# A decode kernel's row change: layer 1 one V tile earlier, and longer FFN steps

## The chip, the cores and the metric

The kernel runs on one core of one Trainium2 chip. The metric is the device time of one execution in microseconds (us). Each kernel was timed beside the kernel before on the same chip, in alternating rounds.

Words used below. PE is the engine of the matrix products, DVE and ACT are the vector and the scalar engine, SP issues the loads; PSUM is the buffer that products are written to. A *tile* is the keys (K) or values (V) of two heads of one batch row, 2 MB. A *unit* is a quarter of a tile, 512 KB, 4 KB in each of 128 partitions. The *arena* is the SBUF buffer of 26 units into which all cache data is loaded. A *visit* is the work on two heads of one row in one layer. A *turn* is the stretch in which layer 0 of a row ends, its feed-forward network (FFN) runs, and layer 1 of that row starts; there are eight. A *gap* is the place in PE's instruction order between the products of two units, where the planner puts small work.

## The reference, cut to what matters

```python
# B=8 rows, one token each, D=640, 32 heads of 128, 4096 cached keys, Dff=1728, bf16
x = A_x
x = x + attention(layernorm(x), k_cache, v_cache, wq, wo)     # layer 0
x = x + relu(layernorm(x) @ w1) @ w2
x = x + attention(layernorm(x), k_cache, v_cache, wq, wo)     # layer 1: same cache, same weights
x = x + relu(layernorm(x) @ w1) @ w2
```

Both layers read the same cache of 537 MB. Layer 1 of a row needs the whole of layer 0 and the FFN of that row first. Rows do not depend on each other, so while row b is between its layers, the kernel works on the first heads of row b+1.

## The kernel before

A planner in Python writes one list of operations for all engines ahead of time. The parts that matter are cut out here ("# ..." marks cuts).

```python
UNIT = 4; G = 26; SPARE = 5; STASH = 3; AHEAD = 2; CAP = 20

def plan(B, NP, n_up, n_down):
    # visits: 16 visits of layer 0 of row b+1, of which the first AHEAD=2 come before layer 1 of row b
    # ...
    keep = set(first[: G - SPARE])               # 21 units stay in the arena from layer 0 for layer 1
    stash = first[G - SPARE : G - SPARE + STASH] # 3 more are copied aside
    slots = []
    for i in range(NV + 1):
        pair = [("K", i)] * (i < NV) + [("V", i - 1)] * (i >= 1)
        ends = i and visits[i - 1][0] == 0 and last_of[visits[i - 1][:2]] == i - 1
        turns = 0 < i < NV and visits[i][0] == 1 and visits[i - 1][0] == 0
        slots += pair[::-1] if ends or turns else pair
    # ...
    def release(which, i, g):      # PE is done with a unit: its place is free, and feed() issues loads
        # ... kept units of layer 0 are not freed
        owner[u], freed[u] = False, at[1]
        # ...
        feed()

    def step():                    # one gap: the next piece of every open chain, up to CAP products
        n, now = 0, []
        for c in sorted(chains, key=lambda c: c[0][0]):
            if not n or n + c[0][0] <= CAP:
                n += c[0][0]; now.append(c)
        # ...

    def finish(layer, b):          # the FFN of a row as a chain of steps (number of products, name)
        # ...
        for k in range(n_up):      # 5 steps of 15 products
            c += [own(15, "up", k)]
            # ...
        c += [own(0, "relu")] + [own(14, "down", k) for k in range(n_down)] + [own(0, "add")]
        c += [own(2, "mean"), own(0, "center")] + query(b, 0)   # next query of the row
        c += [own(1, "var2"), own(0, "root2")] + query(b, 1)
        return c

# the loads and the products of a K unit near a turn
def do_load(b, p, n, u):
    nc.sync.dma_start(out=arena[:, u * GW : (u + n) * GW], in_=A_kv[b, :, p * GW : (p + n) * GW])
# ... keys as weights: 16 products of 128x128 by 128x1 a unit
for n in range(4 * c, 4 * c + 4):
    nc.tensor.matmul(s_tiles[i][:, j : j + 1], lhsT=arena[:, at + n * P : at + (n + 1) * P],
                     rhs=qo[:, b, h : h + 1], start=True, stop=True)
```

What this makes of a turn: 21 units of the row that is ending stay in the arena for layer 1, which saves loading them again. Only 5 places are left for the stream. From the first tile ahead until layer 1 starts to free kept units, each load waits for PE to finish the unit five places back. I call this the *ring*. I call *lead* the time from the issue of a load (the end of the instruction that issues it) to the landing of the load ahead of it: it says how much work the DMA engines still have queued when the new load arrives. In the plan a middle turn (row 1) runs: K tiles of two visits ahead (8 gaps), V tile of the first, V tile of the second, then layer 1's first K tile, which is kept.

Of the kernel before, what the change touches and what calls it, by code (L numbers as in the profile page):

```python
# [22 lines left out]
SOON = 4  # L23
PACE, LATE = 0.6, 2
PAD = 2048
AHEAD = 2
BANK = 512
CAP = 20


def tile_at(NP, which, hp):

    return max(0, 2 * hp - 1) if which == "K" else min(2 * hp + 2, 2 * NP - 1)


def plan(B, NP, n_up, n_down):



# [5 lines left out]
    visits = [(0, 0, hp) for hp in order0]  # L45
    for b in range(B - 1):
        nxt = [(0, b + 1, hp) for hp in order0]
        cur = [(1, b, hp) for hp in order1]
        if b + 1 < B - 1:
            visits += nxt[:AHEAD] + cur + nxt[AHEAD:]  # L50
        else:
            visits += nxt[:AHEAD] + cur[: NP - AHEAD] + nxt[AHEAD:] + cur[NP - AHEAD :]
    visits += [(1, B - 1, hp) for hp in order1]
    NV = len(visits)
    assert NV == 2 * B * NP and NP % GP == 0
    turns = [visits.index((1, b, order1[0])) for b in range(B)]
    moving = [not any(t - AHEAD - 1 <= i < t + 5 for t in turns) and i < NV - 2 for i in range(NV)]
    last_of = {(layer, b): v for v, (layer, b, hp) in enumerate(visits)}
    direct = [i == NV - 1 or visits[i][0] == 0 and last_of[visits[i][:2]] == i for i in range(NV)]
    ahead = [next((t - i for t in turns if 0 < t - i <= AHEAD), 0) for i in range(NV)]  # L60

# [7 lines left out]
    slots = []  # L69
    for i in range(NV + 1):  # L70
        pair = [("K", i)] * (i < NV) + [("V", i - 1)] * (i >= 1)
        ends = i and visits[i - 1][0] == 0 and last_of[visits[i - 1][:2]] == i - 1
        turns = 0 < i < NV and visits[i][0] == 1 and visits[i - 1][0] == 0
        slots += pair[::-1] if ends or turns else pair
    stream, uses = [], []
    for which, i in slots:
        layer, b, hp = visits[i]
# [17 lines left out]
    ops, chains, done = [], [], set()  # L95
# [81 lines left out]
    def step():  # L177
# [3 lines left out]
        for c in sorted(chains, key=lambda c: c[0][0]):  # L181
            if not n or n + c[0][0] <= CAP:
                n += c[0][0]
# [11 lines left out]
    def query(b, n):  # L195

        return [(10, ("Q", b, order1[n])), (0, ("QC", b, order1[n]))]
# [9 lines left out]
    def finish(layer, b):  # L207

        def own(n, *op):
            return n, ("C", layer, b, *op)  # L210

        c = []
        for k in range(n_up):
            c += [own(15, "up", k)]
            if layer:
                c += [own(0, "relu", k)]
            elif k == min(1, n_up - 1):
                c += [own(0, "var"), own(0, "root")]
        if layer:
            for k in range(n_up):  # L220
                c += [own(15, "down", k)] + [own(0, "var"), own(0, "root")] * (k == n_up // 2)
            return c + [own(0, "add")]
        c += [own(0, "relu")] + [own(14, "down", k) for k in range(n_down)] + [own(0, "add")]
        c += [own(2, "mean"), own(0, "center")] + query(b, 0)
        c += [own(1, "var2"), own(0, "root2")] + query(b, 1)
        return c

    feed()
    for which, i in slots:
        layer, b, hp = visits[i]  # L230
# [66 lines left out]
def kernel(  # L297
# [15 lines left out]
    B, Sq, D = A_x.shape  # L313
    H = A_wo.shape[1] // D
    NP = H // 2
    Dh = A_kv.shape[1]
    W = (A_kv.shape[2] - PAD) // (2 * NP)
    Sk = W // 2
    Dff = B_w1.shape[1] // (D // P)
    assert Sq == 1 and Dh == P and D % P == 0 and W % (UNIT * P) == 0  # L320
    DC = D // P
# [6 lines left out]
    FC = (Dff + P - 1) // P  # L328
# [73 lines left out]
    ends = consts.tile([P, 2, B, DC], BF16, name="ends")  # L402
# [18 lines left out]
    assert len(stash) > DC  # L421
    nc.vector.memset(o_ps, 0.0)

    up_parts = [range(f, min(f + 3, FC)) for f in range(0, FC, 3)]
    visits, moving, direct, ahead, ops = plan(B, NP, len(up_parts), DC)
    s_tiles, P_rows, P_tiles, m_tiles, o_tiles, oy, invL, oT, nmax, st = ({} for _ in range(10))

    def first_norm(xln):
# [61 lines left out]
    def over_partitions(out, t):  # L490
        for k in range(2):
            nc.tensor.matmul(out, lhsT=ones_p, rhs=t[:, :, k], start=(k == 0), stop=(k == 1))
# [38 lines left out]
    def finish_steps(layer, b):  # L531




        b0, nb = (b, 1) if layer == 0 else (0, B)
        x = xT[:, b0 : b0 + nb, :]
        if layer:
            h = [(ffn_ps if k % 2 else s_ps)[:, : FC * nb].rearrange("p (f b) -> p f b", b=nb) for k in range(len(up_parts))]
            y = stash_ps.bitcast(FP32).rearrange("p (c n) -> p c n", n=BANK)[:, :DC, :nb]  # L540
        else:
            h = [ffn_ps[:, :FC].rearrange("p (f b) -> p f b", b=1)] * len(up_parts)
            y = ffn_ps[:, FC * B : FC * B + DC].rearrange("p (c b) -> p c b", b=1)

        def up(k):
            for f in up_parts[k]:
                fs = f_sizes[f]
                for c in range(DC):
                    nc.tensor.matmul(
                        h[k][:fs, f, :], lhsT=w1_sb[:, c, f * P : f * P + fs], rhs=st["xf"][:, :, c],  # L550
                        start=(c == 0), stop=(c == DC - 1),
                    )

        def var():
            over_partitions(var_ps[:, :nb], st.pop("s2"))

        def var2():
            over_partitions(var2_ps, st.pop("s2"))

        def root():  # L560
            if layer:
                st["rstd"] = root_of_all(var_ps[:, :nb])
            else:
                st["rstd"] = sm.tile([P, 1], FP32, name="rstd", bufs=1)
                inverse_root(st["rstd"], var_ps[:, :1], 1.0)

        def relu(k=None):
            if not k:
                st["hT"] = temp([P, nb, FC], BF16, "hT").rearrange("p b f -> p f b")
            part = range(FC) if k is None else up_parts[k]  # L570
            for rows, lo, hi in ((P, part[0], min(part[-1] + 1, n_full)), (Dff % P, n_full, part[-1] + 1)):
                if rows and lo < hi:
                    nc.vector.tensor_scalar(
                        out=st["hT"][:rows, lo:hi], in0=h[k or 0][:rows, lo:hi], scalar1=0.0, scalar2=None, op0=ALU.max
                    )

        def down(k):
            for c, f in [(k, f) for f in range(FC)] if layer == 0 else [(c, f) for f in up_parts[k] for c in range(DC)]:
                fs = f_sizes[f]
                nc.tensor.matmul(  # L580
                    y[:, c, :], lhsT=w2_sb[:fs, f, c * P : (c + 1) * P], rhs=st["hT"][:fs, f, :],
                    start=(f == 0), stop=(f == FC - 1),
                )

        def add():
            yT = y.rearrange("p c b -> p b c")
            if layer == 0:
                nc.vector.scalar_tensor_tensor(out=x, in0=yT, scalar=st["rstd"], in1=x, op0=ALU.mult, op1=ALU.add)
                s1 = sm.tile([P, 1], FP32, name="s1", bufs=1)
                nc.vector.tensor_reduce(out=s1, in_=x, axis=AX.X, op=ALU.add)  # L590
                st["s1"] = halves(s1, "s1h")
                return
            t = temp([P, nb, DC], FP32, "ffn")
            nc.vector.tensor_tensor(out=t, in0=yT, in1=_free(st["rstd"], [(1, nb), (0, DC)]), op=ALU.mult)
            nc.vector.tensor_tensor(out=outT, in0=x, in1=t, op=ALU.add)

        def mean():
            over_partitions(mean2_ps, st.pop("s1"))

        def center():  # L600
            xc = sm.tile([P, 1, DC], FP32, name="xc", bufs=1)
            nc.vector.scalar_tensor_tensor(
                out=xc, in0=_free(mean2_ps, [(1, 1), (0, DC)]), scalar=-1.0 / D, in1=x, op0=ALU.mult, op1=ALU.add
            )
            xlns[b] = sm.tile([P, 1, DC], BF16, name="xq", bufs=2)
            nc.vector.tensor_copy(out=xlns[b], in_=xc)
            st["s2"] = halves(squares(xc), "s2h")

        def root2():
            r = q_scale[b] = sm.tile([P, 2], FP32, name="q_scale", bufs=2)  # L610
            inverse_root(r[:, 0:1], var2_ps, float(Dh))
            nc.gpsimd.tensor_scalar(out=r[:, 1:2], in0=r[:, 0:1], scalar1=-1.0, scalar2=None, op0=ALU.mult)

        return dict(up=up, var=var, root=root, relu=relu, down=down, add=add, mean=mean, center=center, var2=var2, root2=root2)
# [58 lines left out]
    def do_mm(which, i, g, u):  # L673
# [19 lines left out]
        for c in range(4):  # L693
            if moving[i]:
# [5 lines left out]
                continue  # L700
            s_tiles[i] = o_ps[:, 2 * NJ : 4 * NJ] if ahead[i] == AHEAD else s_ps[:, i % 2 * 2 * NJ : (i % 2 + 1) * 2 * NJ]
            h = 2 * hp + c // 2
# [164 lines left out]
def _laid_out(A_x, A_k_cache, A_v_cache, A_wq, A_wo, B_w1, B_w2):  # L867
# [12 lines left out]
    for hp in range(NP):  # L880
        kv[:, :, tile_at(NP, "K", hp)] = k[:, hp]
        kv[:, :, tile_at(NP, "V", hp)] = v[:, hp]
    kv = np.pad(kv.reshape(B, p, -1), ((0, 0), (0, 0), (0, PAD)))
    return {
# [32 lines left out]
```

## Time and profile before

Before: 2340.57 us median of 3 runs (2338.99 to 2340.59). Lines of the page of the kernel before (the head and parts 2, 3, 4 and 6; part 2 has 40 slices of some 59 us; the last line tells loads of one unit, their number and the median time from issue to landing):

```profile
span 2343.0 us, 43024 instructions
...
GB/s 411 430 433 401 433 432 432 431 396 432 432 432 430 404 434 431 430 427 403 433 432 431 426 412 434 430 432 420 427 431 427 432 416 430 431 431 431 396 433 329
DMA packets 76753, 990.87 MB, mean 423 GB/s; under 512 B 8596, under 2 KB 8596, under 8 KB 36500
...
q8 instruction: 146, 2.39, 0.4%
...
DMA 71%; PE 17%; ACT 6%; DVE 3%; issue 2%; SPq 0%; POOL 0%; ACTq 0%; DVEq 0%; POOLq 0%
...
arena<-in_A_kv_dram SPq DMA_DIRECT2D x218, 512.0 KB, 6.5
```

DMA bounds the kernel: the chain of waits is 71% arrival of data, and the rate is 426 to 434 GB/s in the slices without a turn, the first and the last slice aside. The Trainium skill, "DMA: Bandwidth & Descriptors", section Specifications, gives a fabric ceiling of 435 GB/s, and the trace agrees with it: no slice is over 434. The rate falls to 396 to 420 in eight dips: these are the turns.

The page has no view of landings, so I computed a table from the DMA records of the trace: for each load its landing (the last of its 16 completions), the time since the landing before, the lead, and the *spread* (from the first to the last of its 16 completions). The same skill page, section "Why a DMA increments its semaphore by 16 and not by 1", says that up to 16 engines finish a transfer independently and that only the full 16 means that the data landed. The trace shows the engines finishing apart: over its 124 loads of 4 MB the spread is 3.1 us in the median (2.1 to 3.9 us in the middle four fifths), and it stood at 5.2 us just before row 1's turn. So some engines run a few us ahead of the slowest one. A unit of a long load costs 1.209 us, so the 1884.6 units of data would take 2278 us. I call *ring loss* the sum, over the one-unit loads of all eight turns, of the time between landings less 1.209 us per unit: 25.9 us for this trace.

Row 1's turn of the kernel before, from that table (us; output of my own reading of the trace, not a view of the profile):

```text
landed   since last  lead   spread
490.38      1.26     10.73   5.23    last load that waited for no place
491.61      1.23      4.03   2.74    ring: 5 places
492.86      1.25      4.00   2.35
494.10      1.24      4.00   1.75
495.36      1.26      3.99   1.48
497.96      2.60      3.98   2.84    an instruction packet of 16 KB started at 495.36
499.19      1.23      5.36   2.33
```

In the ring the lead is 4.0 us, and the landings come 1.25 us apart: PE is not late. Then one landing is 1.4 us late. At that moment the instruction queue (q8 above: 146 packets of 16 KB in the whole run) moved a packet. It takes about 0.94 us of one DMA engine. In this trace all 24 ring landings that were more than 0.3 us late had such a packet near (in the 3 us before the previous landing or since it); they sum to 19.8 us. The test is a wide one: 45% of the ring-bound landings that were on time (one unit, lead under 7.5 us) pass it too, so one late landing near a packet shows little, and it is 24 of 24 that tells. The rings hold 39 of the 146 packets; the other 107 fell elsewhere, where all losses, measured as ring loss is, sum to 25.9 us.

PE in this turn, from the timeline of the kernel before (start, duration, what; L705 is a K unit, L687 a V unit, L549 and L580 are the FFN's up and down products):

```profile
492.62 0.63 PE L549 MATMUL small_ps<-xf,w_sb 128*128 128x1 bf16 x10 [0.26 <-ACT nmax L757]
493.18 0.59 PE L705 MATMUL s_ps<-qo,arena 128*128 128x1 bf16 x16
493.64 0.60 PE L580 MATMUL small_ps<-hT,w_sb 128*128 128x1 bf16 x14
494.18 0.58 PE L705 MATMUL s_ps<-qo,arena 128*128 128x1 bf16 x16
494.62 0.60 PE L580 MATMUL small_ps<-hT,w_sb 128*128 128x1 bf16 x14
```

A gap holds 14 down products in 0.6 us, and the K unit itself holds PE some 0.45 us until the next can start. PE's waits in that turn (486 to 510 us) are mostly for data; the waits view has who waited for whom, total us, times, longest:

```profile
PE o_ps L687 <- DMA arena<-in_A_kv_dram: 1.8, 3, 1.3
PE o_ps L705 <- DMA arena<-in_A_kv_dram: 0.8, 3, 0.3
PE small_ps L655 <- DVE oT L812: 0.3, 1, 0.3
```

### The profile page before, as it was taken

The numbers are of one execution on the slowest core, as the hardware profiler recorded it, in microseconds if no ns is written. First come the engines' busy times: TensorE is split into PE (matmuls) and PEld (weight loads), VectorE is DVE, ScalarE is ACT, GpSimd is POOL, SyncE is SP. The second block draws the span as 40 slices with busy tenths as digits, with TensorE's granted clock in tenths as the row PEclk, the third lists the DMA queues.
The fourth block names the chain that finished last, engine by engine and source line by source line (L and its number), as shares of the span: only waits on it lengthen the run. The fifth ranks groups of instructions, "written<-read, shape, count | busy, mean of one in ns | idle before, by whom it ended". The sixth has DMA issues, their size and how long they took to land.

```text
span 2343.0 us, 43024 instructions
## 1 busy us (share of the span) xinstructions
PE 1398.6 (60%) x18748; PEld 591.4 (25%) x18748; DVE 496.7 (21%) x2022; ACT 426.3 (18%) x986; POOL 59.5 (3%) x296
## 2 busy tenths in 40 slices
PE   3547654576545764557545675556755567545766
PEld 1214211152111511125111241113411133111523
DVE  1113211131112211122111221112211122111312
ACT  1111211122111221112211121111211112111211
POOL 0000000000000000000000000000000000000000
PEclk9999999999999998555555555555555555555555
DMA  9999999999999999999999999999999999999997
GB/s 411 430 433 401 433 432 432 431 396 432 432 432 430 404 434 431 430 427 403 433 432 431 426 412 434 430 432 420 427 431 427 432 416 430 431 431 431 396 433 329
DMA packets 76753, 990.87 MB, mean 423 GB/s; under 512 B 8596, under 2 KB 8596, under 8 KB 36500
## 3 DMA queue, kind: packets, MB, share of 16 engines
q1 hardware_dynamic: 76564, 988.12, 99.4%
q8 instruction: 146, 2.39, 0.4%
q14 instruction: 43, 0.35, 0.0%
HBM read 988.08 MB, written 0.01 MB: 422 GB/s over the span
## 4 chain that ended last, share of the span: by engine, by line
DMA 71%; PE 17%; ACT 6%; DVE 3%; issue 2%; SPq 0%; POOL 0%; ACTq 0%; DVEq 0%; POOLq 0%
DMA arena<-in_A_kv_dram 71%; PE o_ps L687 5%; PE s_ps L695 4%; PE s_ps L705 2%; ACT P_row L755 2%; ACT o_sb L795 1%; PE small_ps L655 1%; DVE mrow L713 1%; ACT P_sb L761 1%; PE small_ps L800 1%; ACT arena L634 1%; PE small_ps L768 1%; PE small_ps L825 1%; DVE hmx L732 0%; ACT nmax L753 0%
## 5 line engine op out<-in xcount | busy, mean ns | idle before, releaser
L687 PE MATMUL o_ps<-arena,P_sb 128*4 128x512 bf16 x3952 | 584.3, 596 | 402.0 <-DMA arena<-in_A_kv_dram 401.0
L695 PE MATMUL s_ps<-arena,qz 128*4 128x512 bf16 x3040 | 410.3, 602 | 261.1 <-DMA arena<-in_A_kv_dram 249.5
L687 PEld LDWEIGHTS <-P_sb 128*4 128x4 bf16 x3952 | 107.4, 88 | 502.8 <-issue 491.7
L713 DVE TENSOR_REDUCE mrow<-s_ps 100x1 bf16<-100x512 f32 x190 | 131.8, 694 | 323.2 <-PE s_ps L695 323.2
L795 ACT CAST o_sb<-o_ps 100x512 bf16<-100x512 f32 x247 | 144.9, 587 | 289.3 <-PE o_ps L687 286.0
L753 ACT ACTIVATE nmax<-small_ps 100x1 f32<-100x1 f32 x106 | 18.1, 171 | 774.5 <-PE small_ps L742 774.5
L775 DVE CAST P_sb<-small_ps 128x64 bf16<-128x64 f32 x190 | 42.6, 224 | 523.1 <-PE small_ps L768 523.1
L695 PEld LDWEIGHTS <-qz 128*4 128x4 bf16 x3040 | 63.9, 85 | 313.7 <-issue 295.5
L705 PEld LDWEIGHTS <-arena 128*128 128x128 bf16 x4224 | 129.6, 104 | 40.8 <-DMA arena<-in_A_kv_dram 23.4
L705 PE MATMUL s_ps<-qo,arena 128*128 128x1 bf16 x3712 | 123.7, 165 | 17.2 <-ACT P_sb L761 7.6
L768 PE MATMUL small_ps<-few,P_row 100*128 100x16 bf16 x760 | 52.3, 179 | 92.1 <-ACT P_row L755 92.1
L753 ACT ACTIVATE nmax<-small_ps,q_scale 100x1 f32<-100x1 f32 x84 | 22.0, 261 | 398.7 <-PE small_ps L742 398.7
L787 DVE TENSOR_REDUCE lsum<-small_ps 128x2 f32<-128x64 f32 x240 | 53.9, 224 | 171.9 <-PE small_ps L781 171.9
L768 PEld LDWEIGHTS <-P_row 100*128 100x128 bf16 x760 | 35.0, 107 | 186.5 <-ACT P_row L755 178.2
L720 PE MATMUL small_ps<-few,mrow 100*1 100x16 bf16 x190 | 34.4, 181 | 67.6 <-DVE mrow L713 67.6
L755 ACT ACTIVATE P_row<-s_ps,nmax 100x512 bf16<-100x512 f32 x106 | 72.8, 687 | 3.4
L800 PEld LDWEIGHTS <-o_sb 100*128 100x128 bf16 x988 | 45.7, 106 | 107.2 <-ACT o_sb L795 73.8
L655 PE MATMUL small_ps<-xq,wq_sb 128*128 128x1 bf16 x1200 | 48.8, 165 | 38.9 <-DVE qo L812 33.5
L800 PE MATMUL small_ps<-few,o_sb 100*128 100x2 bf16 x988 | 65.1, 170 | 10.7 <-DVE lsum L787 2.2
L727 DVE TENSOR_REDUCE diag<-small_ps 1x2 bf16<-1x16 f32 x190 | 30.8, 162 | 186.9 <-PE small_ps L720 186.9
L720 PEld LDWEIGHTS <-mrow 100*1 100x1 bf16 x190 | 15.0, 79 | 210.8 <-DVE mrow L713 210.8
L755 ACT ACTIVATE P_row<-s_ps,nmax,q_scale 100x512 bf16<-100x512 f32 x84 | 65.3, 778 | 2.8
(225 smaller groups left out, 958.0 us busy)
## 6 DMA issues: line engine op xcount, KB each, us to landing
arena<-in_A_kv_dram SPq DMA_DIRECT2D x124, 4096.0 KB, 23.1
arena<-in_A_kv_dram SPq DMA_DIRECT2D x98, 2048.0 KB, 22.7
arena<-in_A_kv_dram SPq DMA_DIRECT2D x218, 512.0 KB, 6.5
arena<-in_A_kv_dram SPq DMA_DIRECT2D x48, 1024.0 KB, 11.3
arena<-in_A_kv_dram SPq DMA_DIRECT2D x11, 3072.0 KB, 22.4
arena<-in_A_kv_dram SPq DMA_DIRECT2D x11, 2560.0 KB, 20.5
arena<-in_A_kv_dram SPq DMA_DIRECT2D x10, 1536.0 KB, 19.7
wq_sb<-in_A_wq_dram SPq DMA_DIRECT2D x4, 1280.0 KB, 17.6
```

Source lines behind the costliest of these rows:

```text
L655: nc.tensor.matmul(q_ps[:, h : h + 1], lhsT=wq_sb[:, g, c, (2 * n + h) * Dh : (2 * n + h + 1) * Dh], rhs=xlns[b][:, 0, c : c + 1], start=( ...
L687: nc.tensor.matmul(o_ps[32 * c : 32 * c + CJ, :], lhsT=P_tiles[i][:, h, j : j + CJ], rhs=arena[:, at + c * CJ * Dh : at + (c + 1) * CJ * D ...
L695: nc.tensor.matmul(s_ps[32 * c : 32 * c + CJ, :], lhsT=qz[:, i % 3, c // 2, 3 - g : 3 - g + CJ], rhs=arena[:, at + c * BANK : at + (c + 1) ...
L705: nc.tensor.matmul(s_tiles[i][:, j : j + 1], lhsT=arena[:, at + n * P : at + (n + 1) * P], rhs=qo[:, b, h : h + 1], start=True, stop=True,)
L713: nc.vector.tensor_reduce(out=m_tiles[i][:OR, :1], in_=s_ps[:OR], axis=AX.X, op=ALU.max)
L720: nc.tensor.matmul(turn_ps[:1, : 4 * CJ], lhsT=m[:OR, :1], rhs=rsel[:OR], start=True, stop=True)
L755: nc.scalar.activation(out=P_rows[i][:OR], in_=s_ps[:OR], func=ACT.Exp, bias=nm[:OR, :1], scale=more)
L768: nc.tensor.matmul(P_ps[:, k * 4 * CJ : (k + 1) * 4 * CJ], lhsT=P_row[:OR, k * P : (k + 1) * P], rhs=rsel[:OR], start=True, stop=True,)
L775: nc.vector.tensor_copy(out=P_tiles[i].rearrange("p h (c k) -> p h c k", k=BANK // P), in_=P_ps.rearrange("p (k h c) -> p h c k", k=BANK / ...
L787: nc.vector.tensor_reduce(out=L, in_=(lsum2_ps if ahead[i] else lsum_ps).rearrange("p (h j) -> p h j", h=2), axis=AX.X, op=ALU.add)
L795: nc.scalar.copy(out=o_tiles[i][:OR], in_=o_ps[:OR, :].rearrange("p (j d) -> p j d", j=CJ))
L800: nc.tensor.matmul(oy[i][:, :2], lhsT=o_tiles[i][:OR, j, :], rhs=gsel[:OR, j, :], start=(j == 0), stop=(j == CJ - 1))
```

## The change

The intent: layer 1's first K tile is already in the arena and is freed as it is used. If it comes one V tile earlier, four units fewer go through the narrow ring. The price is that the FFN and the next query must be done in 12 gaps instead of 16, so the FFN's steps get longer.

```diff
+UPS, DOWNS = 4, 2
+LAST = 3
-CAP = 20
+CAP = 34
@@ plan
-        turns = 0 < i < NV and visits[i][0] == 1 and visits[i - 1][0] == 0
-        slots += pair[::-1] if ends or turns else pair
+        slots += pair[::-1] if ends else pair
@@ finish (layer 0)
-        for k in range(n_up):
-            c += [own(15, "up", k)]
-            ...
-        c += [own(0, "relu")] + [own(14, "down", k) for k in range(n_down)] + [own(0, "add")]
+        for f in range(0, n_f, UPS):
+            c += [own(n_c * min(UPS, n_f - f), "up", f // UPS)] + [own(0, "var"), own(0, "root")] * (f == 0)
+        c += [own(0, "relu")]
+        for k in range(0, n_c, DOWNS):
+            c += [own(n_f * min(DOWNS, n_c - k), "down", k // DOWNS)]
... (layer 1's FFN keeps its steps of 3 tiles; up() and down() follow the new sizes)
```

Order of the two kernels in the plan, row 1's turn (K48 x4: the products of the four units of visit 48's K tile; "L1" is layer 1):

```text
before: K48 x4  K49 x4  V48 x4  V49 x4  L1 K50 x4        ups 15,15,15,15,10  downs 14 x5
after:  K48 x4  K49 x4  V48 x4  L1 K50 x4  V49 x4        ups 20,20,20,10     downs 28,28,14
```

The last turn (row 7) keeps its tile order. Nothing is added in arithmetic, bytes or instructions. One-unit loads fall from 218 to 187.

More of the change, by code (lines that the diff above doesn't have):

```diff
@@ L25, with plan @@
 PAD = 2048
+UPS, DOWNS = 4, 2
+LAST = 3
 AHEAD = 2
 BANK = 512
-CAP = 20
+CAP = 34
 def tile_at(NP, which, hp):
     return max(0, 2 * hp - 1) if which == "K" else min(2 * hp + 2, 2 * NP - 1)
-def plan(B, NP, n_up, n_down):
+def plan(B, NP, n_f, n_c):
     order0 = list(range(NP))
@@ L212, in finish @@
         c = []
-        for k in range(n_up):
-            c += [own(15, "up", k)]
-            if layer:
-                c += [own(0, "relu", k)]
-            elif k == min(1, n_up - 1):
-                c += [own(0, "var"), own(0, "root")]
-        if layer:
-            for k in range(n_up):
-                c += [own(15, "down", k)] + [own(0, "var"), own(0, "root")] * (k == n_up // 2)
-            return c + [own(0, "add")]
-        c += [own(0, "relu")] + [own(14, "down", k) for k in range(n_down)] + [own(0, "add")]
-        c += [own(2, "mean"), own(0, "center")] + query(b, 0)
+        if layer:
+            n = -(-n_f // LAST)
+            for k in range(n):
+                c += [own(15, "up", k), own(0, "relu", k)]
+            for k in range(n):
+                c += [own(15, "down", k)] + [own(0, "var"), own(0, "root")] * (k == n // 2)
+            return c + [own(0, "add")]
+        for f in range(0, n_f, UPS):
[3 more added lines that the diff above has]
+            c += [own(n_f * min(DOWNS, n_c - k), "down", k // DOWNS)]
+        c += [own(0, "add"), own(2, "mean"), own(0, "center")] + query(b, 0)
         c += [own(1, "var2"), own(0, "root2")] + query(b, 1)
@@ L422 @@
     nc.vector.memset(o_ps, 0.0)
-    up_parts = [range(f, min(f + 3, FC)) for f in range(0, FC, 3)]
-    visits, moving, direct, ahead, ops = plan(B, NP, len(up_parts), DC)
+    visits, moving, direct, ahead, ops = plan(B, NP, FC, DC)
     s_tiles, P_rows, P_tiles, m_tiles, o_tiles, oy, invL, oT, nmax, st = ({} for _ in range(10))
@@ L536, in finish_steps @@
         b0, nb = (b, 1) if layer == 0 else (0, B)
+        n = LAST if layer else UPS
+        up_parts = [range(f, min(f + n, FC)) for f in range(0, FC, n)]
         x = xT[:, b0 : b0 + nb, :]
@@ L577, in down @@
         def down(k):
-            for c, f in [(k, f) for f in range(FC)] if layer == 0 else [(c, f) for f in up_parts[k] for c in range(DC)]:
+            cs = range(k * DOWNS, min((k + 1) * DOWNS, DC))
+            for c, f in [(c, f) for c in cs for f in range(FC)] if layer == 0 else [(c, f) for f in up_parts[k] for c in range(DC)]:
                 fs = f_sizes[f]
```

## The prediction

> **What bounds the kernel now.** DMA. The page gives 990.87 MB at a mean of 423 GB/s in 2343.0 us; DMA is 9 in every slice but the last, PE is 60% busy, and the chain of waits is 71% arrival of cache tiles. The Trainium skill, "DMA: Bandwidth & Descriptors", section Specifications, gives a fabric ceiling of 435 GB/s; the trace agrees: stretches of 32 KB packets run at 432.
>
> From the trace's DMA records: a unit (512 KB, a quarter tile) of a long load costs 1.209 us, so 1884.6 units need 2278 us. The other 62: some 9 at the start, 10 after the last tile, 6 because the 218 one-unit loads have 4 KB packets (1.24 us a unit), and about 37 in some 45 late landings, nearly all beside a packet of the instruction queue (146 of 16 KB, 0.94 us each). In long loads the 16 completions of one load spread over about 5 us, so other engines absorb such a hit. In a turn (layer 0 of a row ends, its FFN runs, layer 1 starts) 21 of the arena's 26 units are kept for layer 1; loads go one unit at a time round 5 places, the spread falls to 1.5 to 2.8 us, and a hit delays everything by 0.5 to 1.4. Eight turns hold some 24 of the 37 us.
>
> PE does not starve the DMA there: in row 1's turn each load is issued 4.0 us before the one ahead lands, and PE waits 0.2 to 0.3 us per unit for the tile (timeline).
>
> **The change** adds no arithmetic, byte or instruction. In rows 0 to 6 layer 1's first K tile, which is kept, moves ahead of the second V tile, so four units fewer go round the ring: one-unit loads fall from 218 to 187, all loads from 521 to 496. The FFN must finish in 12 gaps instead of 16: five ups of 15 products become 20, 20, 20, 10; five downs of 14 become 28, 28, 14.
>
> Estimates from trace durations: 15 ups take 0.54 us (27 ns each), so 20 take 0.68; 14 downs take 0.61 (33 ns), so 28 take 1.07. A K unit holds PE 0.45 us. Up gaps stay under 1.25 us; the two gaps with 28 downs come to 1.5, so PE falls back by 0.5 us and the issue lead dips to about 3.3 us before the V gaps recover it. No starvation, but less room for the spread.
>
> **On the critical path** is ring time, not FFN work. Fewer one-unit loads save 1 us. A turn's ring shrinks from about 20 units to 16: a fifth of the 24 us goes, 4 to 5. The longer gaps give back 1 or 2. Net 4 us, uncertain by several from where instruction packets fall.
>
> **Predicted: 2336 us, range 2329 to 2342; faster by over 2% 0.01, within 2% 0.97, slower by over 2% 0.02.**
>
> **Right would show** as 146 instruction packets again, 187 loads of 512 KB, mean GB/s up by about 1, low turn slices shorter, late landings in turns summing to 18 to 21 us, start and end as before. **Wrong on the PE side**: PE waits for DVE (ReLU, add) grow, loads in the turn are issued under 2 us before the one ahead lands, or one-unit landings stand over 1.3 us apart with no instruction packet near.
>
> **What would make it wrong.** If the chain add, mean, centre, query misses its 12 gaps, PE stalls before layer 1's first product while the DMA runs dry (1 to 3 us a turn). If the shorter ring lets the spread rebuild, more hits are absorbed and the gain is 10 us.

## The result, and the profile after

After: 2349.89 us median of 6 runs (2348.31 to 2352.01). Before, in the same rounds: 2340.58 us median of 6 (2338.99 to 2343.26). Ratio 1.004, 95% interval 1.0027 to 1.0052. A ratio is the mean time of one kernel's runs over that of the other's in the same rounds, so it is not quite the ratio of the medians. The change costs 9.3 us, 0.4%, where a gain of 4.6 us was predicted. It is clear of noise, and outside the range of the prediction.

The same lines of the page after:

```profile
span 2348.1 us, 42958 instructions
...
GB/s 411 430 432 398 435 428 435 430 397 434 431 432 427 400 431 433 431 428 401 430 433 432 424 409 430 431 431 417 415 431 432 433 402 425 430 432 430 400 433 336
DMA packets 73153, 990.86 MB, mean 422 GB/s; under 512 B 8197, under 2 KB 8197, under 8 KB 32133
...
q8 instruction: 146, 2.39, 0.4%
...
DMA 71%; PE 18%; ACT 5%; DVE 4%; issue 2%; SPq 0%; DVEq 0%; ACTq 0%; POOL 0%; POOLq 0%
...
arena<-in_A_kv_dram SPq DMA_DIRECT2D x187, 512.0 KB, 6.9
```

The granted clock of PE differed between runs (0.556 to 1.0), but it explains none of the 9 us: the one run of this kernel at 1.0 took 2348.31 us, 0.2 under the next of its six; one of the kernel before at 1.0 (in the rounds of section 8) took 2341.69, where the others took 2338 to 2343.

The parts that the prediction counted came out: 146 instruction packets, 187 one-unit loads. From the landing of the last cache load to that of the output it is 9.6 us in both traces. The outcome did not: the dips of the GB/s line are as deep as before or slightly deeper (398, 397, 400 and 401 against 401, 396, 404 and 403 in the first four), and the mean went from 423 to 422. (The profiled run of before took 2344.78 us, some 4 us over its median, so the two pages differ by 5 us where the medians differ by 9.)

My sum by stage, from the landing tables: losses outside the turns, measured as ring loss is, are 25.9 us before and 25.1 after; ring loss rose from 25.9 to 31.4 us, though the ring has 181 loads in place of 208. What changed in kind: in the trace before, no late ring landing was without an instruction packet near; in the trace after, 8 of 26 were, 5.6 us in all. All late landings in the turns sum to 24.5 us, where the prediction named 18 to 21.

Row 1's turn after, from the landing table:

```text
landed   since last  lead   spread
495.18      1.23      4.00   1.89
496.39      1.21      3.99   1.86
498.20      1.81      3.49   1.75    a packet started at 495.13
499.42      1.23      3.65   1.76
500.64      1.21      3.34   1.74
502.74      2.10      3.02   1.99    a packet started at 501.10
504.26      1.52      3.96   1.94    the same packet, within the 3 us of the test
505.95      1.69      3.67   1.61    no instruction packet near
507.19      1.24      4.69   1.64
```

The lead has fallen to 3.0. The timeline after shows why (L709 is a K unit, L552 and L584 are the FFN's up and down products, L659 the query):

```profile
491.40 0.63 PE L552 MATMUL small_ps<-xf,w_sb 128*128 128x1 bf16 x10 [0.37 <-DVE hmx L736]
491.96 0.59 PE L709 MATMUL s_ps<-qo,arena 128*128 128x1 bf16 x16
492.40 1.15 PE L584 MATMUL small_ps<-hT,w_sb 128*128 128x1 bf16 x28
...
493.60 0.59 PE L709 MATMUL s_ps<-qo,arena 128*128 128x1 bf16 x16
494.05 1.15 PE L584 MATMUL small_ps<-hT,w_sb 128*128 128x1 bf16 x28
495.14 0.58 PE L709 MATMUL s_ps<-qo,arena 128*128 128x1 bf16 x16
496.04 0.24 PE L785 MATMUL s_ps<-P_sb,few 128*128 128x64 bf16 x1 [0.32 <-DVE mrow L719]
496.09 0.63 PE L584 MATMUL small_ps<-hT,w_sb 128*128 128x1 bf16 x14
...
499.29 0.41 PE L659 MATMUL s_ps<-xq,wq_sb 128*128 128x1 bf16 x10 [0.76 <-ACT P_sb L765]
```

K units start at 491.96, 493.60 and 495.14: 1.64 and 1.54 us apart, where a unit's load takes 1.25. A gap with 28 downs holds PE 1.15 us, on top of the unit's 0.45. The third, with 14 downs, is no shorter, because PE waits 0.32 us for a reduction on DVE. Then the query at 499.29 sits 0.76 us idle. In this turn's issue times the six gaps from 491.2 to 500.6 us are 1.71, 1.65, 1.53, 1.54, 1.17 and 1.81 us long, 9.4 us in place of 7.4 at a unit's pace (1.23): five of the six are slow, and PE falls 2.0 us behind. PE's waits in 486 to 510 us after:

```profile
PE s_ps L659 <- ACT P_sb L765: 0.8, 1, 0.8
PE small_ps L659 <- DVE oT L816: 0.6, 2, 0.3
PE o_ps L709 <- DMA arena<-in_A_kv_dram: 0.4, 2, 0.2
```

They have turned from waits for data into waits for the other engines (ACT and DVE): PE is now the late one.

### The profile page after: what moved, and what is told of

Read it like the earlier page. It is cut to its first block, busy times and chain, and to the rows that moved or that the text cites. A ratio compares the mean times of both kernels' runs of the same rounds, so it can differ in the third digit from the quotient of the medians.

```text
span 2348.1 us, 42958 instructions
## 1 busy us (share of the span) xinstructions
PE 1387.7 (59%) x18748; PEld 590.7 (25%) x18748; DVE 496.9 (21%) x2022; ACT 425.3 (18%) x986; POOL 59.0 (3%) x296
## 4 chain that ended last, share of the span: by engine, by line
DMA 71%; PE 18%; ACT 5%; DVE 4%; issue 2%; SPq 0%; DVEq 0%; ACTq 0%; POOL 0%; POOLq 0%
DMA arena<-in_A_kv_dram 71%; PE o_ps L691 5%; PE s_ps L699 4%; PE s_ps L709 3%; ACT P_row L759 2%; ACT o_sb L799 1%; PE small_ps L659 1%; PE small_ps L804 1%; DVE mrow L717 1%; ACT P_sb L765 1%; PE small_ps L584 1%; PE small_ps L772 1%; PE small_ps L829 1%; DVE hmx L736 1%; ACT arena L638 1%
## 5 line engine op out<-in xcount | busy, mean ns | idle before, releaser
L691 PE MATMUL o_ps<-arena,P_sb 128*4 128x512 bf16 x3952 | 573.9, 596 | 497.1 <-DMA arena<-in_A_kv_dram 496.9
L709 PEld LDWEIGHTS <-arena 128*128 128x128 bf16 x4224 | 129.7, 104 | 25.9 <-DMA arena<-in_A_kv_dram 18.5
L709 PE MATMUL s_ps<-qo,arena 128*128 128x1 bf16 x3712 | 123.4, 165 | 7.0 <-DMA arena<-in_A_kv_dram 4.8
L659 PE MATMUL small_ps<-xq,wq_sb 128*128 128x1 bf16 x1200 | 48.7, 165 | 38.1 <-DVE qo L816 33.6
L659 PEld LDWEIGHTS <-wq_sb 128*128 128x128 bf16 x1280 | 53.5, 104 | 51.1 <-issue 51.0
## 6 DMA issues: line engine op xcount, KB each, us to landing
wq_sb<-in_A_wq_dram SPq DMA_DIRECT2D x4, 1280.0 KB, 28.9
```

The lines of the kernel that those rows point to most:

```text
L659: nc.tensor.matmul(q_ps[:, h : h + 1], lhsT=wq_sb[:, g, c, (2 * n + h) * Dh : (2 * n + h + 1) * Dh], rhs=xlns[b][:, 0, c : c + 1], start=( ...
L691: nc.tensor.matmul(o_ps[32 * c : 32 * c + CJ, :], lhsT=P_tiles[i][:, h, j : j + CJ], rhs=arena[:, at + c * CJ * Dh : at + (c + 1) * CJ * D ...
```

## The experiments

Sixteen kernels ran. Theory A: the changed kernel loses because PE is late in the ring, so loads are issued late, the lead falls, and the DMA engines lose time. Theory B: the new tile order costs by itself. Theory C: instruction packets simply fall elsewhere. Theory D came later: long PE steps cost by themselves, and the lead is only a sign.

Variants with the old order were made from the changed kernel by putting the two `turns` lines back; with the old step sizes such a plan differs from the kernel before in 40 of its 6401 operations (where `var` and `root` stand in the chain).

### 1. The new order alone

```diff
-UPS, DOWNS = 4, 2
+UPS, DOWNS = 3, 1
-CAP = 34
+CAP = 20
```

> The new tile order with the old FFN steps (5 ups of 15, 5 downs of 14, cap 20). Theory A (the long FFN steps make PE late in the ring, the issue lead falls from about 3.9 to 3 us, and each hit of an instruction packet then costs more): 2335 to 2340 us, least leads of the turns back at 3.6 or more. Theory B (the order itself costs: layer 1 comes before its inputs are ready): 2346 to 2352 us, like the changed kernel. Theory C (neither; instruction packets just fall elsewhere): anything from 2335 to 2352.

Measured: 2347.91 us (2344.89 to 2351.74, 5 runs) against 2341.33 (9 runs of before); ratio 1.003, interval 1.0018 to 1.0043. The order alone costs 6.6 us, even with the old step sizes. Theory A as I stated it, with all of the loss in the steps, is wrong; theory B is alive. The least leads of the turns were 2.2 to 3.7 us, so the lead had fallen here too. The profiled run was the fastest of the five, so its ring loss (24.2 us) understates the kernel.

### 2. The new steps alone

```diff
+        turns = 0 < i < NV and visits[i][0] == 1 and visits[i - 1][0] == 0
-        slots += pair[::-1] if ends else pair
+        slots += pair[::-1] if ends or turns else pair
```

> The old tile order with the new FFN steps (20, 20, 20, 10 and 28, 28, 14, cap 34). Theory A: 2346 to 2352 us, ring losses up by about 1 us a turn, least leads near 3. Theory B: 2340 us, as before. Theory C: anything from 2335 to 2352.

Measured: 2351.49 us (2350.41 to 2353.41, 5 runs); ratio 1.0045, interval 1.0033 to 1.0058. The long steps alone cost 10 us, as theory A expects and theory B does not. Ring loss 32.1 us, least leads 2.5 to 3.3 in rows 1 to 6, and 6.3 us of late landings with no packet near. The two halves do not add: steps 10, order 6.6, both 9.3.

### 3. The new order with downs of 14

```diff
-UPS, DOWNS = 4, 2
+UPS, DOWNS = 4, 1
```

> The new order with ups of 20 but downs of 14 (no gap with 28 products), cap 34. Theory A: 2335 to 2341 us, because no gap of PE is longer than the 1.25 us of a unit's load. Theory B: 2346 to 2352 us. Theory C: anything from 2335 to 2352.

Measured: 2346.76 us (2345.33 to 2352.67, 5 runs); ratio 1.0029, interval 1.0015 to 1.0042. That is above the range of theory A and like the order alone: it agrees with a cost of the order, not with the 28 downs as the only cause.

### 4. A strong dose on the old order

```diff
-UPS, DOWNS = 4, 2
+UPS, DOWNS = 14, 5
   (old order, as in 2)
```

> Strong dose on the old order: all 70 ups in one gap and all 70 downs in the next, the same products and instructions in number. Theory A: the lead falls to about 1.5 us for several units, 2350 to 2365 us. Theory B: 2338 to 2343 us. Theory C: no relation to the dose.

Measured: 2370.24 us (2369.76 to 2370.59, 4 runs); ratio 1.0125, interval 1.0111 to 1.0139. The cost follows the dose: 28.9 us, more than expected. Products, bytes and instruction packets are the same in number. Least leads were -0.7 to 1.7 us (below zero: the DMA queue had run empty), ring loss 54.0 us. Page lines of this kernel:

```profile
span 2368.7 us, 43014 instructions
...
GB/s 413 430 430 374 434 431 433 429 380 433 430 433 429 389 432 430 432 427 389 434 430 433 417 400 432 431 432 387 416 431 428 434 385 427 430 432 430 382 433 332
...
q8 instruction: 146, 2.39, 0.4%
```

The slices of the turns fall to 374 to 389 GB/s, while the slices between them stay at 430 to 434, and the instruction queue is at 146 packets as ever. The time is lost in the turns.

### 5. Controls: the kernel before again, and shifted instruction packets

> Control: the kernel before, unchanged, against itself. All theories: ratio 1.000 within 0.001, about 2341 us. Its profile gives a second reading of the ring losses and the lead in the turns, beside which the others are judged.

Measured: 2339.8 us (2339.18 to 2342.35, 5 runs); ratio 0.9995, interval 0.9981 to 1.0009. Ring loss 25.0 us: a second trace of the same kernel agrees with the first within 1 us.

```diff
+        for n in range(64):
+            nc.tensor.matmul(turn_ps[:, :1], lhsT=ident[:, :2], rhs=ident[:, :1], start=True, stop=True)
         first_norm(xln0)
```

> The kernel before with 64 tiny products (128 PE instructions) added at its start: later PE instructions, and with them the fetches of the instruction queue, fall elsewhere, half a fetch of 256 instructions further if a fetch brings 256. Theory C (the differences of 6 to 10 us come from where the fetches fall): a change of 5 us or more either way. Theory A: within 3 us of before.

Measured: 2340.15 us (2338.74 to 2342.51, 5 runs); ratio 0.9996, interval 0.9984 to 1.0009. Moving the packets by half a fetch changes nothing that can be seen. This one shift speaks against theory C, and the doses in 2, 4 and 6 do not need it.

### 6. The lead without touching PE: the number of ring places

```diff
-SPARE = 5
+SPARE = 4        # spare4;  SPARE = 6 for spare6
```

With 4, the kernel keeps 22 units and copies 2 aside, 24 in all as before, so it loads the same bytes; tile order and FFN steps are those of before. With 6 it keeps 20 and copies 3, so one unit a row more is loaded.

> The kernel before, one line: SPARE 4 in place of 5, so 22 units are kept and 2 stashed (24 in all, as before: the same bytes) and the ring has 4 places. PE's steps and the tile order are untouched. Theory A (what costs time is the issue lead in the ring): the lead falls from 4.0 to about 2.75 us, in-turn losses rise by 1 to 3 us a turn, 2349 to 2365 us. Rival D (long PE steps cost by themselves, the lead is only a sign): 2339 to 2343 us.

> The kernel before with SPARE 6: 20 kept and 3 stashed, so 8 units more are loaded (9.7 us at 1.21 us each), and the ring has 6 places. Theory A: the lead rises to about 5.2 us and the in-turn losses fall by 3 to 8 us in all: 2343 to 2348 us. Rival D: 2349 to 2352 us.

Measured for 4 places: 2372.04 us (2369.61 to 2373.29, 4 runs) against 2341.14; ratio 1.0132, interval 1.0118 to 1.0146. That is far from what rival D expects, and 7 us above the range of theory A: the sign is as expected, the size larger. In row 1's turn the first ring load has a lead of 2.75 us and a spread of 1.33 us (before: 4.03 and 2.74). Ring loss is 56.0 us, of which 17.3 are late landings with no packet near (here 53% of the late landings and 46% of those on time have one near, so packets hardly tell them apart). Page lines with 4 places:

```profile
span 2370.5 us, 42949 instructions
...
GB/s 412 431 430 371 433 431 432 431 387 433 430 433 427 376 433 432 433 426 379 434 432 432 413 392 432 432 432 401 410 432 432 432 398 419 431 431 430 378 430 338
```

Measured for 6 places: 2345.22 us (2343.9 to 2346.73, 5 runs); ratio 1.0019, interval 1.0006 to 1.0032. Eight units more at 1.209 us are 9.7 us, but the time grew by 4.1: the larger lead (5.2 us) gave some 5.6 us back. Ring loss is 13.7 us, and every late landing has a packet near. Page lines with 6 places:

```profile
span 2342.1 us, 42985 instructions
...
GB/s 412 429 433 414 431 433 434 428 416 427 432 432 429 415 434 430 432 427 411 434 431 433 426 415 431 435 430 421 425 433 431 431 413 429 429 434 430 413 432 340
```

The dips in the first slice with a turn: 371 GB/s with 4 places, 401 with 5, 414 with 6. This shows that the cause theory A names is enough: with PE's steps, the tile order and the bytes as before, a place less, and with it 1.25 us less lead, costs 31 us. (The one-unit loads also rise from 218 to 229; at some 0.03 us each, 1.24 us a unit in place of 1.21, that is under 1 us.)

```diff
-SPARE = 5        # in the changed kernel
+SPARE = 6
```

> The changed kernel with SPARE 6 likewise. Theory A: with a place more the long steps no longer eat into what the DMA engines need; within 4 us of the old order with SPARE 6, so the 9 us between the two kernels mostly close. Rival D: 8 to 10 us above it.

Measured: 2353.16 us (2352.03 to 2355.43, 5 runs); ratio 1.0053, interval 1.0041 to 1.0066. It is 7.9 us above the old order with 6 places: the gap did not close, against what I expected of theory A. The landing table says this much: in row 1's turn the lead starts at 5.2 us and falls to 3.7, where I had expected PE to be 0.5 us late. PE's lateness (issue gaps of 1.82, 1.65, 1.53, 1.53, 1.17 and 1.81 us, 2.1 us over the pace) eats the added place and more. Row 1 itself loses little (1.7 us against 1.3). Ring loss is 22.0 us against 13.7 in all, and 5.9 of the difference lies in rows 0, 2 and 3, where the least leads are 2.7 to 3.1 us (with the old order 3.9 to 4.3); but row 5, with a least lead of 2.8, lost no more than there. So this run does not tell D from A by itself; together with 4 places, where PE's steps are untouched and the loss is three times as large, D alone cannot be the cause.

### 7. PE's wait for the FFN's tail

In both kernels the products for mean, second variance and query read results of DVE and ACT. Here they read constants and the first norm, so those waits for data go. Their outputs are wrong, which doesn't matter for the times.

```diff
-            over_partitions(mean2_ps, st.pop("s1"))
+            st.pop("s1")
+            over_partitions(mean2_ps, ident[:, :2].rearrange("p (a b) -> p a b", a=1))
   (the same for var2)
-                    rhs=xlns[b][:, 0, c : c + 1], ...
+                    rhs=xln0[:, b, c : c + 1], ...
```

> Wrong results on purpose. Old order, old step sizes, but the products for mean, second variance and query read constants and the first norm, so that PE does not wait for add, mean and centre. Theory A2 (what the new order lost is PE waiting for this chain just ahead of layer 1's first K tile): 2338 to 2342 us, as before, since the old order has room for the chain. Theory B (the order itself): the same.

Measured: 2340.18 us (2338.46 to 2342.33, 5 runs); ratio 0.9996, interval 0.9984 to 1.0009. In the old order the chain costs nothing.

> Wrong results on purpose. As the one with small steps in the new order (2347.9 us), but with the chain's products reading constants, as above. Theory A2: 2336 to 2341 us, least leads over 3.5 us, the loss against before gone. Theory B: still 2345 to 2350 us.

Measured: 2344.78 us (2341.67 to 2346.4, 5 runs); ratio 1.0013, interval 1.0 to 1.0026. Between the two expectations: 3.5 us over before where the order with its chain was 6.6 over, with overlapping intervals. Least leads are still 2.9 to 3.7 in rows 1 to 7.

> Wrong results on purpose: the changed kernel, but the products of mean, second variance and query read constants, so PE does not wait for add, mean and centre. If the waits for this chain are part of PE's lateness: 2343 to 2347 us, 3 to 6 below the changed kernel's 2350. If only the long steps count: 2348 to 2352 us.

Measured: 2347.49 us (2346.47 to 2349.6, 5 runs) against 2340.85; ratio 1.0028, interval 1.0016 to 1.0041. That is 6.6 us over before instead of 9.3, as expected if the waits are a part, but again the intervals (1.0016 to 1.0041, and 1.0027 to 1.0052) overlap. The long steps remain the larger part.

```diff
-        dst = qz[:, i % 3, :, 3] if moving[i] else qo[:, b, 2 * hp : 2 * hp + 2]
+        dst = qz[:, i % 3, :, 3] if moving[i] else qz[:, i % 3, :, 7]      # columns that nothing reads
   (new order, small steps, and the edit above)
```

> Wrong results on purpose: new order, small steps, chain products on constants, and the query's copy goes to columns that nothing reads, so layer 1's first K tile waits for nothing but its own data. If the new order's last 3 us (2344.8 against 2341.2) are PE's wait for query and copy just ahead of that tile: 2337 to 2342 us, the saving of four ring units seen at last. If the order has another cost, or no saving: 2343 us or more.

Measured: 2346.66 us (2344.37 to 2349.76, 5 runs); ratio 1.0026, interval 1.0014 to 1.0039. A miss. Its timeline shows that the edit did not take PE's waits away: between 1648.8 and 1650.4 us the products for the softmax sum, mean, query and layer 1's first K unit still alternate with DVE and ACT. All four write to one PSUM tile (`s_ps`), and PE waits for the reader of the last one, 0.32, 0.26 and 0.26 us. The lead still falls to 2.9 us at that K tile. Whether the new order would gain if PE were on time there is open.

### 8. Which long step

```diff
-UPS, DOWNS = 4, 2
+UPS, DOWNS = 4, 1    # ups20_old, CAP = 20;  UPS, DOWNS = 3, 2 for downs28_old, CAP = 34 (old order)
```

> Old order, ups of 20, 20, 20, 10, downs still of 14. The gaps with 20 ups were estimated under the 1.25 us of a unit's load. If only gaps over 1.25 us cost: 2339 to 2343 us, share of ring loads with a lead under 3.5 us at 0.03 or less. If any longer step costs: 2344 us or more.

Measured: 2344.15 us (2342.11 to 2348.98, 5 runs); ratio 1.0014, interval 1.0001 to 1.0028. Just over the border I had set; 10% of the ring loads have a lead under 3.5 us, against 1 to 3% before.

> Old order, ups of 15, downs of 28, 28, 14. If the long downs are the costly part of the steps: 2346 to 2352 us, share of ring loads with a lead under 3.5 us above 0.1. If they need the longer ups as well: 2340 to 2344 us.

Measured: 2348.57 us (2347.22 to 2351.06, 5 runs); ratio 1.0033, interval 1.0021 to 1.0046. The 28 downs are the larger part, 8 us; the 20 ups may cost 3. Together they measured 10.

### 9. A try at a faster kernel

```diff
-    moving = [not any(t - AHEAD - 1 <= i < t + 5 for t in turns) and i < NV - 2 for i in range(NV)]
+    moving = [not any(t - AHEAD - 1 <= i < t + 2 for t in turns) and i < NV - 2 for i in range(NV)]
```

> A try at a faster one: the kernel before, with the first five visits of layer 1 that use keys as weights cut to two (the others stream the keys past the query, 8 PE instructions a unit in place of 32). 2064 PE instructions fewer, so 8 instruction packets fewer if a packet brings 256 instructions: 138 in place of 146, and 2336 to 2340 us. If the packets have nothing to do with PE's instruction count: 146 again.

Measured: 2346.43 us (2345.41 to 2348.48, 5 runs); ratio 1.0027, interval 1.0014 to 1.0041. Slower, against the expectation, but the packets did fall. The queue's line on its page:

```profile
q8 instruction: 138, 2.26, 0.3%
```

2064 PE instructions fewer made 8 packets fewer, 258 instructions a packet. The Trainium skill, "Runtime: NRT & Kernel Launch", section "Instruction fetch mechanics", says that each engine's instruction memory is refilled in blocks of 16 KiB, 256 instructions, through a DMA queue of its own; for PE, the only engine whose count was changed, the trace agrees. The ring loss was no higher (21.2 us); losses in the 40 us after each ring were 13.4 us in place of 6.8. The cause stays open. No kernel tried beats the kernel before.

### All runs beside each other

From the landing tables, all traces: the share of ring-bound loads (one unit, lead under 7.5 us) that were issued with a lead under 3.5 us; ring loss in us; the part of it in late landings (over 0.3 us) with no instruction packet near; and the measured ratio to before.

```text
kernel        order steps             places  share<3.5  ring loss  no packet  ratio
spare6        old   15 / 14           6       0.00       13.7       0.0        1.0019 (8 units more to load)
old_free      old   15 / 14           5       0.03       19.1       0.0        0.9996
before_shift  old   15 / 14           5       0.01       20.0       0.5        0.9996
before_again  old   15 / 14           5       0.02       25.0       0.4        0.9995
before        old   15 / 14           5       0.03       25.9       0.0        1
moving2       old   15 / 14           5       0.02       21.2       1.0        1.0027
order_small   new   15 / 14           5       0.12       24.2       1.2        1.0030
order_4_1     new   20 / 14           5       0.15       25.2       3.5        1.0029
order_free    new   15 / 14           5       0.12       25.8       5.8        1.0013
order_free2   new   15 / 14           5       0.11       27.9       5.4        1.0026
ups20_old     old   20 / 14           5       0.10       27.1       2.5        1.0014
downs28_old   old   15 / 28           5       0.10       30.5       3.8        1.0033
after_free    new   20 / 28           5       0.13       29.6       1.5        1.0028
after         new   20 / 28           5       0.19       31.4       5.6        1.0040
steps_old     old   20 / 28           5       0.18       32.1       6.3        1.0045
after_spare6  new   20 / 28           6       0.13       22.0       5.0        1.0053 (8 units more to load)
lump_old      old   70 / 70           5       0.22       54.0       8.2        1.0125
spare4        old   15 / 14           4       0.40       56.0      17.3        1.0132
```

One trace stands behind each row, and two traces of one kernel differ by about 1 us, of near-equal kernels by 6. The large rows stand well clear of that.

Two more readings of these traces. First, ring loss accounts for the time where the cause is strong: against the trace of before (2343.0 us), steps_old is 5.6 us longer with 6.2 more ring loss, lump_old 25.7 with 28.1, spare4 27.5 with 30.1. For the new order with short steps the differences are no larger than those among traces of near-equal kernels, so they settle nothing. Second, the DMA engines do run short of work. Over the stretches of ring-bound loads, the share of the 16 engines' time without a packet is -1.9% with 6 places, -1.6 to -0.7% in the old order with old steps (packet records overlap a little, so it can fall below zero), 0.9 to 1.3% in the four kernels with steps of 20 / 28, 2.5% in spare4 and 7.2% in lump_old. In the new order with short steps (order_small, order_free, order_free2) it is -0.6 to -0.1%, between the two.

## Why the prediction was wrong

**Right.** DMA bounds the kernel, what the change altered sits in the turns, the start and the tail stayed, 146 packets and 187 one-unit loads. The sign named for a failure on the PE side is what came: one-unit landings over 1.3 us apart with no instruction packet near, 0 us before and 5.6 us after in late landings. The other sign, an issue lead under 2 us, did not: 2.2 us (in row 0, as before) was the least, and 2.7 to 3.4 us in the other rows. PE's waits for DVE in row 1's turn grew from 0.9 to 1.3 us, but not those for ReLU and add.

**Wrong: "PE falls back by 0.5 us and the issue lead dips to about 3.3 us before the V gaps recover it."** The single terms were close (28 downs took 1.15 us where 1.07 was estimated), but the sum was mis-sized. I counted two long gaps and free recovery. The trace has five slow gaps among six in a row, 2.0 us late in row 1: the gap of the last 10 ups also holds a wait for DVE, the gap after the 28s waits for a reduction, and the query waits 0.76 us in the V gaps where I expected recovery. Taking the chain's waits for data out measured 6.6 us over before instead of 9.3 (intervals overlap).

**Wrong: "No starvation, but less room for the spread", "the longer gaps give back 1 or 2."** This is the step that turned the sign. The long steps alone cost 10 us. A lead of 4.0 us looked like 4 us of slack, and I took half a microsecond less as nearly free. It is not slack. As I read it, it lets the fast DMA engines go on while the slowest one catches up; the engines' time without a packet, above, fits this, but no run watched single engines. What is shown is the price: with one place less (lead 2.75 us, same bytes, same PE steps) the kernel lost 31 us; with one more it gained back some 5.6.

**Wrong: "a fifth of the 24 us goes, 4 to 5".** I scaled the loss with the number of units in the ring. The ring did shrink, from 208 loads to 181, but the instruction packets that fell into the rings did not: 39 before, 38 after, because they come with PE's instructions, and PE does the same work in a shorter ring. Late landings near a packet cost 19.8 us before and 18.9 after.

**Wrong: "On the critical path is ring time, not FFN work."** Through the ring, FFN work is on it: PE frees the place that the next load waits for.

**Open.** Why the new order with old step sizes costs 3 to 7 us and does not gain. Its lead falls to 2.9 us at layer 1's first K tile in several turns, which fits theory A, but the two runs that were to take PE's waits away there left some in place (one PSUM tile), so no run shows the order with PE on time.

## What to carry to other kernels

Where a load waits for the place that an engine frees, measure the time from issue to the landing ahead: that lead is a resource. Here 1.25 us less of it cost 31 us, although no ring load found the queue empty (the least lead with 4 places was 0.7 us). Before making steps longer in such a stretch, add up every gap of the engine with its waits on other engines, and compare the sum with the pace of the loads; a few tenths over in five gaps of a turn, in eight turns, came to some 10 us here. A loss that comes with events (here instruction fetches) does not shrink with the length of the stretch unless the events leave it.

## What the Trainium skill lacked or had wrong

- "Runtime: NRT & Kernel Launch", section "Instruction fetch mechanics", calls the cost of crossing a 16 KiB block of instructions mostly hidden. It has no word on what the fetch takes from a kernel whose DMA engines are full: the fetches' packets took 0.94 us each of a DMA engine, and in the eight rings of the kernel before the landings that were late beside such a packet sum to 19.8 us of 2341. That the packet is the cause of each is inferred from their coincidence; all 24 late landings had one near, against 45% of those on time.
- "DMA: Bandwidth & Descriptors" has no word on how far ahead loads must be issued to keep the engines full. Here, with 512 KB loads, a ring of 4 places (lead 2.75 us at its start) measured 1.0132 of the time of a ring of 5 (lead 4.0 us), at the same bytes.
- "DMA: Bandwidth & Descriptors", Specifications, puts the least transfer for line rate at 512 B. The rate still rises above that: in the trace before, the median packet of 4 KB takes 159 ns and the median one of 32 KB 1213 ns, which is 25.8 against 27.0 GB/s an engine, so 4 KB is still 4.6% short.
